# An S4 convolution block and a gated MLP on one core: LayerNorm arithmetic taken off GpSimd, inverse transforms in other PSUM banks, a new schedule

## The chip, the cores and the metric

One core of a Trainium2 chip runs the whole program as one launch. The metric is device time in microseconds (us). The kernel before takes 370.67 us (median of 3 runs, 370.54 to 370.81). Engines in the profile: PE is TensorE (PEld its weight loads), DVE is VectorE, ACT is ScalarE, POOL is GpSimd, SP the queue that issues DMAs. In these traces an engine takes its instructions in the order of its queue: in the kernel before, ACT stood still for 6.19 us behind one result from GpSimd. The order is fixed when the kernel is built: a list scheduler places instructions by priorities that the kernel gives it.

All runs quoted are of the undisturbed state.

## The reference, cut to what matters

```python
def reference(A_u, A_A_re, ..., B_w_gate, B_w_up, B_w_down):
    x = A_u                                      # 1 x 2048 x 640, bf16
    h  = x + _A_ref(_layernorm(x), ...)          # per-channel convolution with a kernel of 2048 taps
    h2 = h + _B_ref(_layernorm(h), ...)          # (sigmoid(ln @ w_gate) * (ln @ w_up)) @ w_down, F = 1728
    return h2
# _A_ref: K = Re(sum_n C exp(dt A l) dt B); y = irfft(rfft(u) * rfft(K)); y + u * Dskip
```

## The kernel before

The sequence is cut into four blocks of 512. In a **setup** of some 157 us the kernel builds tables (sines and exponentials on ACT, products on DVE), normalises the four input blocks (LayerNorm 1), transforms them (`ps_z`), builds the spectra of the convolution kernel (`pk`, `ps_kv`, `ps_xk`) and finishes block 0. Then comes an **MLP stage** of some 212 us, block by block: gate and up projections, down projection; beside them DVE multiplies spectra for the next block (`products`) and PE transforms them back (`inverse`).

LayerNorm 1 before. Block 3's first three rows are summed on ACT (`SA[3]` is 3), and three tiny operations on 3 columns join the sums on GpSimd. Then GpSimd adds eps, takes the power -1/2, and for rows that ACT normalises also forms -mean*rstd:

```python
def ln_stats_act(src, mv, rr, junk, eng=nc.vector, eps=0.0):      # called with nc.gpsimd for LayerNorm 1
    rs = slice(rr[0], rr[-1] + 1)
    for i, r in enumerate(rr):
        nc.scalar.activation(junk(i), src(r), AF.Identity, accum_out=acc[:, 0, r:r + 1])       # L399
    eng.tensor_scalar(acc[:, 0, rs], acc[:, 0, rs], -1.0 / D, None, ALU.mult)                   # L400
    for i, r in enumerate(rr):
        nc.scalar.activation(junk(i), src(r), AF.Square, bias=acc[:, 0, r:r + 1], accum_out=acc[:, 1, r:r + 1])  # L402
    eng.tensor_scalar(mv[:, rs, 0], acc[:, 0, rs], -1.0, None, ALU.mult)                        # L403
    eng.tensor_scalar(mv[:, rs, 1], acc[:, 1, rs], 1.0 / D, eps, ALU.mult, ALU.add)             # L404

def norm(b):
    rs = slice(4 * b, 4 * b + 4); na = AT["NA"][b]
    nc.gpsimd.tensor_scalar(rstd[:, rs], mv[:, rs, 1], 1e-5, None, ALU.add)                     # L416
    nc.gpsimd.tensor_tensor(rstd[:, rs], rstd[:, rs], mhalf[:, rs], ALU.pow)                    # L417
    if na:
        nc.gpsimd.tensor_tensor(nmr[:, rs], mv[:, rs, 0], rstd[:, rs], ALU.mult)                # L419
        nc.gpsimd.tensor_scalar(nmr[:, rs], nmr[:, rs], -1.0, None, ALU.mult)                   # L420
    # ... the last na rows are normalised on ACT, the others on DVE
```

The inverse of a later block goes through the same two PSUM buffers as the up projection, 320 columns at a time, from chunk 9 of 13 on. Blocks in `R4` combine two half spectra on DVE first (radix 4), so that their inverse needs half the matmuls:

```python
def inverse(b, psp):                      # psp = psu_p, two banks of one buffer each
    for half in range(2):
        for s in range(4):
            ps = psp.tile([P, 512], F32, name="ps_y1", tag="ml_pu")
            for ft in range(1 if b in R4 else 2):
                for ri in range(2):
                    MM(ps[:, 0:UH], lhsT=iv(s, ft, ri), rhs=VR[b][...], ...)
            nc.scalar.copy(tb, ps[:, 0:UH]); V(hv, tb, hv, ALU.add)
            yield
# in the MLP loop:
for ft in range(FT):
    up(pg, Wg, 128 * ft); up(pu, Wu, 128 * ft)       # sigmoid, copy, product follow
    if ft > 8: drain(inv, 2)
```

The numbers in `AT` say when each unit of the setup is offered to the scheduler.

## Time and profile before

| | PE | DVE | ACT | POOL |
|---|---|---|---|---|
| busy us of 371.0 | 330.1 | 289.0 | 246.4 | 25.3 |

The table of busy time by stage and the stall at 42 us are shown in the prediction. Two more rows of the page, each a row of 40 slices of 9.3 us, with the busy share (or the granted clock) in tenths:

```profile
PE   1488649896999989989999999998999999999995
...
POOL 1240453100000000010000100000100001000000
PEclk9999969998999999999999999999999999999999
```

Read them above each other: PE's deepest dip after the first 20 us is in the fifth and sixth slice (6 and 4), where POOL is busiest (4 and 5), and the clock has its lowest digit, 6, in the sixth.

One caution for all comparisons of traces: the traced execution of this kernel took 372.78 us, 2.1 more than its median.

### The profile page before, as it was taken

The numbers are of one execution on the slowest core, as the hardware profiler recorded it, in microseconds if no ns is written. First come the engines' busy times: TensorE is split into PE (matmuls) and PEld (weight loads), VectorE is DVE, ScalarE is ACT, GpSimd is POOL, SyncE is SP. The second block draws the span as 40 slices with busy tenths as digits, with TensorE's granted clock in tenths as the row PEclk, the third lists the DMA queues.
The fourth block names the chain that finished last, engine by engine and source line by source line (L and its number), as shares of the span: only waits on it lengthen the run. The fifth ranks groups of instructions, "written<-read, shape, count | busy, mean of one in ns | idle before, by whom it ended". The sixth has DMA issues, their size and how long they took to land.

```text
span 371.0 us, 6647 instructions
## 1 busy us (share of the span) xinstructions
PE 330.1 (89%) x2587; PEld 206.1 (56%) x2602; DVE 289.0 (78%) x594; ACT 246.4 (66%) x450; POOL 25.3 (7%) x32
## 2 busy tenths in 40 slices
PE   1488649896999989989999999998999999999995
PEld 1375436566867677964445654445654436644463
DVE  2979975897899997989999999999999962111221
ACT  6879659897898974476568855558845468755500
POOL 1240453100000000010000100000100001000000
PEclk9999969998999999999999999999999999999999
DMA  7980000146305216979910044000012000010001
GB/s 189 350 331 18 0 2 0 46 144 238 73 2 133 84 72 202 345 203 329 294 65 3 0 144 141 2 0 0 3 71 73 0 0 2 0 72 1 0 30 43
DMA packets 29217, 34.35 MB, mean 93 GB/s; under 512 B 16385, under 2 KB 24578, under 8 KB 28930
## 3 DMA queue, kind: packets, MB, share of 16 engines
q1 hardware_dynamic: 29186, 33.94, 28.2%
q8 instruction: 20, 0.33, 0.4%
q14 instruction: 11, 0.09, 0.1%
HBM read 24.74 MB, written 9.18 MB: 91 GB/s over the span
## 4 chain that ended last, share of the span: by engine, by line
DVE 31%; PE 28%; issue 17%; ACT 16%; POOL 4%; DMA 3%; SPq 1%; POOLq 0%; DVEq 0%; ACTq 0%
PE ml_po L891 5%; DVE u L675 5%; DVE u L674 5%; PE ps_xk L501 4%; PE ml_pu L861 4%; PE ml_pg L861 4%; DVE u L677 3%; DVE u L678 3%; DVE ml_hm L872 2%; PE ps_z L440 2%; PE ps_kv L470 2%; ACT zs L441 2%; ACT a_cs L267 2%; POOL ln_acc L400 2%; PE pk L459 2%
## 5 line engine op out<-in xcount | busy, mean ns | idle before, releaser
L861 PE MATMUL ml_pg<-lnT,Wg 128*128 128x512 bf16 x250 | 65.2, 379 | 0.5
L861 PE MATMUL ml_pu<-lnT,Wu 128*128 128x512 bf16 x256 | 63.7, 379 | 0.2
L891 PE MATMUL ml_po<-Wd,ml_hm 128*128 128x320 bf16 x416 | 59.5, 299 | 0.0
L891 PEld LDWEIGHTS <-ml_hm 128*128 128x128 bf16 x416 | 40.2, 98 | 17.1 <-issue 1.3
L869 ACT ACTIVATE ml_sg<-ml_pg 128x512 bf16<-128x512 f32 x52 | 31.1, 597 | 27.3 <-PE ml_pg L861 15.2
L871 ACT CAST ml_ub<-ml_pu 128x512 bf16<-128x512 f32 x52 | 30.4, 584 | 20.8 <-PE ml_pu L861 19.8
L861 PEld LDWEIGHTS <-Wu 128*128 128x128 bf16 x260 | 25.4, 98 | 30.9 <-issue 0.3
L872 DVE TENSOR_TENSOR ml_hm<-ml_ub,ml_sg 128x512 bf16<-128x512 bf16 x52 | 21.7, 418 | 24.5 <-ACT ml_ub L871 24.5
L440 PE MATMUL ps_z<-u,c_G 128*128 128x320 bf16 x192 | 31.1, 306 | 10.8 <-ACT tabMB L267 6.6
L861 PEld LDWEIGHTS <-Wg 128*128 128x128 bf16 x260 | 25.4, 98 | 26.7
L501 PE MATMUL ps_xk<-kv,c_KM 128*128 128x160 bf16 x320 | 28.6, 241 | 2.6 <-ACT zs L441 1.9
L440 PEld LDWEIGHTS <-c_G 128*128 128x128 bf16 x192 | 18.6, 99 | 20.7 <-issue 11.2
L675 DVE TENSOR_TENSOR u<-Z,S 128x1280 bf16<-128x1280 bf16 x34 | 27.7, 815 | 0.0
L674 DVE TENSOR_TENSOR u<-Z,S 128x1280 bf16<-128x1280 bf16 x34 | 27.5, 814 | 0.0
L240 PE MATMUL ps_t<-fr,c_dg 128*128 128x160 f16 (+1 forms) x180 | 21.0, 247 | 6.7 <-ACT fr L223 4.9
L501 PEld LDWEIGHTS <-c_KM 128*128 128x128 bf16 x320 | 24.2, 102 | 4.4 <-issue 3.6
L240 PEld LDWEIGHTS <-c_dg 128*128 128x128 f16 x180 | 15.7, 103 | 14.5 <-issue 8.6
L410 POOL TENSOR_TENSOR rstd<-mv,mhalf 128x4 f32<-128x4 f32 x4 | 5.1, 1267 | 235.6 <-DVE mv L404 149.7
L677 DVE TENSOR_TENSOR u<-u,u 128x1280 bf16<-128x1280 bf16 x23 | 18.8, 816 | 0.0
L678 DVE TENSOR_TENSOR u<-u,u 128x1280 bf16<-128x1280 bf16 x23 | 18.8, 816 | 0.0
L441 ACT CAST zs<-ps_z 128x640 bf16<-128x640 f32 x24 | 16.4, 721 | 2.0 <-DMA dz<-zs 1.8
L760 PE MATMUL ps_y<-VR,c_IV 128*128 128x320 bf16 x64 | 15.4, 301 | 2.5 <-ACT ml_ub L871 2.3
(156 smaller groups left out, 582.5 us busy)
## 6 DMA issues: line engine op xcount, KB each, us to landing
dz<-zs SPq DMA_DIRECT2D x12, 320.0 KB, 2.2
c_KM<-s4c_KM SPq DMA_DIRECT2D x1, 2560.0 KB, 12.7
h<-in_A_u_dram SPq DMA_DIRECT2D x4, 640.0 KB, 4.4
dxk<-xk SPq DMA_DIRECT2D x16, 160.0 KB, 2.9
eo<-dz SPq DMA_DIRECT2D x4, 640.0 KB, 4.4
S<-dxk SPq DMA_DIRECT2D x4, 640.0 KB, 5.3
Wg<-in_B_w_gate_dram SPq DMA_DIRECT2D x4, 520.0 KB, 8.2
Wu<-in_B_w_up_dram SPq DMA_DIRECT2D x4, 520.0 KB, 8.1
```

The lines of the kernel that those rows point to most:

```text
L240: MM(ps[:, a, q * w:q * w + w], lhsT=dg[:, dk, :], rhs=fr[:, src, i, o + oo:o + oo + w], start=False, stop=(q == m - 1 and i == 1))
L440: MM(ps[:, ri, 0:UH], lhsT=G[:, ft, 0 if b in EO else hf, ri, r, :], rhs=us[b][:, r, o:o + UH], start=(r == rr[0]), stop=(r == rr[-1]))
L501: mm = MM(ps[:, hf, ri * W:ri * W + W], lhsT=KM[:, ft, hf, ri, KI[d] + q, :], rhs=kv[:, j, :], start=(q == 0), stop=(q == len(KD[d]) - 1)).ins
L674: V(t1, z, k[:, :, :, hs_], ALU.mult)
L675: V(t2, z, k[:, :, ::-1, hs_], ALU.mult)
L677: V(s1, s1, t1, ALU.add)
L678: V(s2, s2, t2, ALU.add)
L861: nc.tensor.matmul(ps[:], lhsT=W[:, dc, f0:f0 + 128], rhs=lnT[:, dc].rearrange("p a b -> p (a b)"), start=(dc == 0), stop=(dc == 4))
L869: nc.scalar.activation(sg[:], pg[:], AF.Sigmoid)
L871: nc.scalar.copy(ub[:], pu[:])
L872: nc.vector.tensor_tensor(hm[:, ft, :], ub[:], sg[:], ALU.mult)
L891: nc.tensor.matmul(po[k][:, c, 0:320], lhsT=hm[:, ft, 128 * lr:128 * lr + 128], rhs=Wd[:, ft, 320 * c:320 * c + 320], start=(start and ft ...
```

## The change

The intent, as the diff lets one read it: because of the port that GpSimd shares with VectorE (the page of the Trainium skill is in the prediction), GpSimd keeps only the operation that VectorE is not used for (the power), and the statistics and coefficients go to VectorE. The inverses leave the up projection's banks for those of the down projection, which are idle until it starts. Block 3 loses radix 4. The down eviction is split in two. Most schedule numbers are new.

```diff
-R4 = (1, 3)
+R4 = (1,)
-AT = {"eb": -20.4, ... "NG": (1, 0, 0, 0), "NA": (0, 3, 3, 1), "SA": (0, 0, 0, 3), ...}
+AT = {"eb": -21.2, ... "NG": (1, 0, 0, 1), "NA": (1, 1, 0, 2), "SA": (2, 0, 0, 3), ...}   # most numbers differ
+    def coef(b):
+        rs = slice(4 * b, 4 * b + 4)
+        nc.vector.tensor_scalar(mv[:, rs, 1], mv[:, rs, 1], 1e-5, None, ALU.add)
+        nc.gpsimd.tensor_tensor(rstd[:, rs], mv[:, rs, 1], mhalf[:, rs], ALU.pow)
     def norm(b):
-        nc.gpsimd.tensor_scalar(rstd[:, rs], mv[:, rs, 1], 1e-5, None, ALU.add)
-        nc.gpsimd.tensor_tensor(rstd[:, rs], rstd[:, rs], mhalf[:, rs], ALU.pow)
         if na:
-            nc.gpsimd.tensor_tensor(nmr[:, rs], mv[:, rs, 0], rstd[:, rs], ALU.mult)
-            nc.gpsimd.tensor_scalar(nmr[:, rs], nmr[:, rs], -1.0, None, ALU.mult)
+            nc.vector.scalar_tensor_tensor(nmr[:, qs], mv[:, qs, 0], -1.0, rstd[:, qs], ALU.mult, ALU.mult)
-            ln_stats_act(..., lambda i: junk[:], nc.gpsimd)
+            ln_stats_act(..., lambda i: junk[:])
-        unit(f"n{b}", f"st{b}", L(norm, b))
+        unit(f"w{b}", f"st{b}", L(coef, b))
+        unit(f"n{b}", f"w{b}", L(norm, b))
     def inverse(b, psp):
-            for s in range(4):
-                ps = psp.tile([P, 512], F32, name="ps_y1", tag="ml_pu")
+            for a in range(2):
+                ps = psp.tile([P, 2, 512], F32, name="ps_y1", tag="ml_po")       # two outputs per tile and eviction
-        inv = inverse(b + 1, psu_p)
+        inv = inverse(b + 1, pso_p)
-            if ft > 8: drain(inv, 2)
+            if ft in (7, 8, 10, 12): drain(inv, 1)
-    # down eviction: one ACT copy and one DVE add of 640 columns
+    # down eviction: for c in range(2): one copy and one add of 320 columns
```

## The prediction

> **What bounds the kernel now.** I read the page first (busy shares and the row of 40 slices), then the table of busy time by stage, then the waits of each engine by stage, and last the timeline of the places that stood out. The page gives TensorE (PE) 330.1 us busy of 371, VectorE (DVE) 289.0, ScalarE (ACT) 246.4, GpSimd (POOL) 25.3. In the table of stages (start:end, length, then busy us of PE, PEld, DVE, ACT, POOL, the PE clock, DMA share, GB/s):
>
> ```profile
> 20.00:40.00 20.00, 16.12 (x121) 12.06 (x121) 17.88 (x40) 17.50 (x24) 3.84 (x4) 1.00 0.33 131
> 40.00:60.00 20.00, 12.47 (x88) 8.50 (x88) 16.82 (x41) 12.42 (x22) 11.88 (x11) 0.83 0.01 1
> 60.00:80.00 20.00, 18.53 (x208) 12.29 (x206) 15.36 (x24) 18.83 (x35) 1.15 (x2) 1.00 0.17 64
> 80.00:100.00 20.00, 17.04 (x219) 14.21 (x217) 16.27 (x39) 16.80 (x35) 0.00 (x0) 0.91 0.50 158
> 100.00:120.00 20.00, 19.13 (x216) 14.82 (x216) 19.87 (x37) 17.42 (x26) 0.00 (x0) 1.00 0.27 68
> ...
> 280.00:300.00 20.00, 19.66 (x91) 8.54 (x91) 19.86 (x39) 10.63 (x20) 0.00 (x0) 1.00 0.04 16
> 300.00:320.00 20.00, 19.54 (x138) 11.90 (x138) 5.67 (x20) 16.82 (x35) 1.01 (x1) 1.00 0.00 1
> ```
>
> From 100 us on PE runs at 18 to 20 of every 20 us at full clock: the gate/up/down matmuls, with the far spectra and the inverses as filling. Time there is PE work, with DVE nearly as full up to 300 us. Before 100 us PE is idle 28.2 us (100 less 7.60, 16.12, 12.47, 18.53, 17.04) and DVE 20.7 us. So a gain has to come mainly from the first 100 us. The worst stage is 40 to 60, the only one where GpSimd is busy for long and the only one before 80 us with the PE clock below 1. The timeline shows why:
>
> ```profile
> 42.37 6.93 POOL L400 TENSOR_SCALAR ln_acc<-ln_acc 128x3 f32<-128x3 f32 x1 [17.29 <-ACT junk L399]
> 49.34 0.83 ACT L402 ACTIVATE junk<-u,ln_acc 128x640 bf16<-128x640 bf16 x1 [6.19 <-POOL ln_acc L400]
> 51.16 2.29 PE L440 MATMUL ps_z<-u,c_G 128*128 128x320 bf16 x8 [6.58 <-ACT tabMB L267]
> 51.14 0.66 DVE L298 TENSOR_TENSOR tabMB<-tabEB,tabMB 128x960 bf16<-128x960 bf16 x1 [1.94 <-ACT tabMB L267]
> ```
>
> One GpSimd multiply of 3 columns takes 6.93 us. ACT, in order, waits 6.19 us for it before the squares of block 3's statistics; a cosine table behind them comes late; PE, needing its PSUM tile, waits 6.58 us. DVE had other work and loses only 1.94 us at once. The debt comes later: before 59.61 us DVE waits 1.2 us for a GpSimd pow of the late block 3 or its neighbour, and in 60 to 80 us 4.6 us in one piece for table A's buffer, held by late PE products.
>
> **What the skill says.** "SBUF — State Buffer", section "Who interferes with whom": GpSimd's SBUF port is DVE's second pair, an exclusive lock; a DVE instruction with two SBUF inputs blocks a GpSimd instruction that reads SBUF. The trace agrees: from 42.97 to 49.2 us DVE ran two-input TENSOR_TENSORs without a gap, and the GpSimd multiply ended at 49.30, when DVE ran dry. The same kind of operation took 0.24 us at 49.38, and the multiply of 1.70 us at 23.37 ended just after a 1.48 us DVE product from 23.51. "TensorE: Matmul & The Clock Gate", section "HAM oscillation — how this bites in real kernels": an idle gap over about 3.4 us drops the clock. Here, after 6.58 idle us, eight 320-column matmuls took 2.29 us against 1.25 us for the eight at 26.94, and two groups of six 160-column matmuls 1.00 us each against 0.58. Same page, "Back-to-back issue gap": N/2.4 + 2.5 ns, so 136 ns at N = 320; the trace has 26 down matmuls in 3.69 us, 142 ns each.
>
> **The change, part by part.**
>
> (1) *GpSimd keeps only pow.* The three operations of L400, L403, L404, four +eps (L416) and three multiply pairs (L419, L420) leave GpSimd; DVE gets some 13 tiny operations, mostly in place of longer GpSimd ones, 0.1 to 0.2 us each (the tiny aggregates of L394 are 0.196), so about +2 us of DVE. The pows stay (L417, 1.05 us each). They can still be blocked, but nearly all that follows a pow is now DVE's own: when DVE reaches the normalisation it stops, the port comes free, and the pow ends in about 1 us. Starvation limits itself. On the path: 6.58 us of PE wait go, and some 1.9 us of slow clock (1.04 for the eight plus 0.42 twice). Together 8.5 us at most. Not all comes back, because DVE must keep up: of its own idle time from 40 to 100 us, waits of 1.94, 1.2, 4.6, 2.1 and 1.4 us, 11.2 us in all, I let the 7.7 us that follow from the stall (1.94 + 1.2 + 4.6) be recoverable, less the 2 us added. I take **5.5 us**.
>
> (2) *New schedule numbers and shares.* Block 0 gets two rows of statistics on ACT, ACT normalises 4 rows instead of 7, and the negation of the last table goes to ACT. DVE: two fewer rows of statistics at 2x0.464 + 0.196 = 1.12 each, -2.2; three more normalised rows at 0.43, +1.3; negation of two half tables, about -1: **-2 us of DVE**, cancelling the addition of (1). ACT: two rows at (0.73 + 0.82 + 2x0.19), +3.9; three rows at 0.926, -2.8; negation at half the 2.39 us of the whole table, twice, +2.4: +3.5 us, on an engine with 36% idle. The order of the whole setup is redone; block 1's normalisation and block 3's forward transform move forward, the last chunk's kernel products back. No row tells what an order is worth. As it was surely searched with (1) in place, and PE still has 15 idle us in 0 to 40, I choose **+1.5 us of gain**.
>
> (3) *Inverses to the down projection's banks.* Eight 320-wide tiles per block in the two-buffer up-projection banks become four 2x320 tiles in banks idle until the down projection, issued after chunks 7, 8, 10 and 12 instead of 9 to 12. PE's waits of L760 on ACT's up evictions, 2.3 us in four, should go. ACT: 24 copies at 0.429 become 12 at 0.682 (the down eviction of the same shape), 10.3 to 8.2; DVE: 24 adds at 0.317 become 12 at 0.486, 7.6 to 5.8. I take **2 us**.
>
> (4) *Block 3 without radix 4.* PE: 4 outputs, 2 halves and 2 products more: 16 more 320-column matmuls at 0.14 = **2.2 us lost** on the bound engine. DVE: 4 x (0.482 + 0.482 + 0.317) = 5.1 us less in products(3), which end near 301 us. That helps only if inverse(3) must not be waited for earlier; PE waits just 0.2 us for VR there now, so I count 0.
>
> (5) *Down evictions in halves.* 12 ACT copies at 0.682 become 24 at 0.429, +2.1 us; 12 DVE adds at 0.486 become 24 at 0.317, +1.8. Both cancel (3)'s savings and lie beside PE's work. At the end, the last 0.82 us add from PSUM becomes two of about 0.45, the first starting one matmul (0.14) earlier: 0 ± 0.1.
>
> Sum: 5.5 + 1.5 + 2 - 2.2 = 6.8 us, less a little for worse fits: 370.7 to about **363.6 us**, -1.9%.
>
> **Rivals.**
> A. *The stall moves.* Pow at block 3 or the new ACT statistics of block 0 wait in turn: ACT now needs DVE to reach a tiny multiply in its own queue, and pow can be starved. For it: pow reads two SBUF inputs; four pows in the second half take 1.0 to 1.5 us and DVE waits about 1 us for each. Against: none of eight pows exceeded 1.51 us. If several waits of 1 to 2 us appear the gain shrinks to some 3 us: 367 to 368.
> B. *DVE becomes the bound.* It is 99% busy from 100 to 120 us and 95 to 100% in every stage from 160 to 300 us, so an earlier PE might just wait for it at the inverses, which now come two chunks earlier. For it: the chain of waits runs almost wholly over DVE from 145 to 260 us. Against: DVE loses 5.1 us of radix 4, and its 20.7 idle us before 100 are of the same order as PE's. If it holds, the stall's gain is halved: 365 to 366.
> C. *The reordering is worth more.* PE has 28 idle us before 100; if the new order uses 5 us more of them, with the stall gone, 358 to 360. Nothing in the profile speaks against it but that the first 27 us wait for loads and the phase computation.
> D. *The extra matmuls bite doubly*, with weight loads exposed where inverses are interleaved (pairs at 0.23 us apart now, around the narrow edge matmuls): 16 x 0.23 = 3.7 us instead of 2.2. It adds 1.5 us.
>
> **Range and chances.** The central sum is 363.6. The terms I chose rather than read, (1)'s share and (2), carry ±3 us each, so about ±5: 358 to 368.5. The line of 2% is 363.3, next to the estimate. Slower by 2% would need a new stall of 14 us, which nothing suggests. Faster 0.48, same 0.50, slower 0.02.
>
> **What would show it.** (1) is right if no GpSimd operation lasts over 2 us, PE's wait on the cosine table is gone, the clock stays 1.00 in 40 to 60 us and PE is busy there for 16 us or more. (2): PE's idle time before 100 us falls from 28 to about 20 us. (3): the inverse matmuls wait under 0.5 us in all. (4): 80 instead of 64 inverse matmuls, 2 us more PE work, DVE through products(3) earlier relative to the end of PE's work. (5): the tail after the last matmul stays near 0.8 us plus the store. It is wrong if PE's idle time before 100 us hardly changes (A), if inverses wait for VR (B), or if far more than 8 us of it goes (C).

## The result

After: 366.11 us median of 4 runs (365.43 to 367.81), beside 370.74 us (370.54 to 370.85, 4 runs) of the kernel before. The ratio is 0.9883 with a 95% interval of 0.9849 to 0.9916: about 1.2% faster, inside 2%. Ratios here are the mean time of one kernel's runs over that of the other's of the same rounds, so not quite the ratio of the medians. The prediction's range, 358.0 to 368.5, holds the result; its central value, 363.6, was 2.5 us too low.

The stage table of the kernel after (columns as in the prediction: start:end, length, busy us of PE, PEld, DVE, ACT, POOL, PE clock, DMA share, GB/s):

```profile
20.00:40.00 20.00, 15.97 (x108) 10.76 (x108) 18.54 (x49) 18.68 (x28) 2.02 (x2) 0.91 0.29 117
40.00:60.00 20.00, 17.64 (x213) 12.43 (x215) 20.00 (x48) 17.73 (x35) 2.75 (x2) 1.00 0.01 2
60.00:80.00 20.00, 16.85 (x160) 11.40 (x149) 19.80 (x42) 18.39 (x36) 0.92 (x1) 1.00 0.43 148
80.00:100.00 20.00, 18.20 (x235) 13.87 (x234) 16.27 (x31) 19.15 (x31) 0.00 (x0) 1.00 0.28 85
...
280.00:300.00 20.00, 20.00 (x103) 9.20 (x102) 10.80 (x22) 11.46 (x21) 0.00 (x0) 1.00 0.00 0
```

From 40 to 60 us PE does 17.64 us of work instead of 12.47, at full clock, and DVE never stops. From 280 to 300 us DVE is done with its products half way through, where it was full before (part of this is only that the whole MLP stage begins 7.3 us earlier, see below). GpSimd's timeline (start us, duration us, engine, line, operation) now holds four powers of LayerNorm 1 and nothing long:

```profile
21.29 1.01 POOL L416 TENSOR_TENSOR rstd<-mv,mhalf 128x4 f32<-128x4 f32 x1 [19.79 <-DVE mv L415]
27.17 1.01 POOL L416 TENSOR_TENSOR rstd<-mv,mhalf 128x4 f32<-128x4 f32 x1 [4.87 <-DVE mv L415]
44.66 1.18 POOL L416 TENSOR_TENSOR rstd<-mv,mhalf 128x4 f32<-128x4 f32 x1 [16.47 <-DVE mv L415]
55.67 1.57 POOL L416 TENSOR_TENSOR rstd<-mv,mhalf 128x4 f32<-128x4 f32 x1 [9.84 <-DVE mv L415]
```

A good marker splits every trace in two: the start of the first power of LayerNorm 2 (L410), after which the MLP stage runs. It stands at 158.83 us before (about 156.7 in a run of median length, if its 2.1 us surplus is taken off) and at 151.51 us after. From there to the end it is 212.17 us before and 212.69 us after. So the whole gain, about 5 us, was made in the setup, and the MLP stage gave half a microsecond back.

### The profile page after: what moved, and what is told of

It is laid out like the page before. It is cut to its first block, busy times and chain, and to the rows that moved or that the text cites. A ratio compares the mean times of both kernels' runs of the same rounds, so it can differ in the third digit from the quotient of the medians.

```text
span 364.2 us, 6687 instructions
## 1 busy us (share of the span) xinstructions
PE 330.4 (91%) x2618; PEld 205.6 (56%) x2618; DVE 284.4 (78%) x594; ACT 249.4 (68%) x457; POOL 11.1 (3%) x19
## 4 chain that ended last, share of the span: by engine, by line
PE 39%; DVE 32%; ACT 20%; issue 3%; DMA 3%; POOL 1%; SPq 1%; POOLq 0%; DVEq 0%; ACTq 0%
PE ml_pg L867 8%; PE ml_pu L867 8%; PE ml_po L900 6%; DVE u L679 5%; DVE u L678 5%; DVE u L682 3%; DVE u L681 3%; ACT zs L444 3%; PE ps_xk L504 2%; DVE ml_hm L878 2%; PE ps_kv L473 2%; PE pk L462 2%; ACT a_sn L267 2%; DVE VR L689 2%; PE ps_z L443 2%
## 5 line engine op out<-in xcount | busy, mean ns | idle before, releaser
L875 ACT ACTIVATE ml_sg<-ml_pg 128x512 bf16<-128x512 f32 x52 | 31.0, 597 | 24.2 <-PE ml_pg L867 16.3
L443 PE MATMUL ps_z<-u,c_G 128*128 128x320 bf16 x192 | 29.1, 298 | 4.7 <-ACT zs L444 2.8
L504 PE MATMUL ps_xk<-kv,c_KM 128*128 128x160 bf16 x320 | 27.1, 232 | 1.9 <-ACT xk L508 0.8
L504 PEld LDWEIGHTS <-c_KM 128*128 128x128 bf16 x320 | 22.8, 98 | 4.3 <-issue 3.0
L462 PE MATMUL pk<-tabB,tabA 128*128 128x84 bf16 x320 | 15.5, 200 | 2.7 <-ACT kts L463 2.6
L462 PEld LDWEIGHTS <-tabA 128*128 128x128 bf16 x320 | 14.0, 97 | 6.0 <-issue 3.6
L463 ACT CAST kts<-pk 128x420 bf16<-128x420 f32 x32 | 15.0, 533 | 2.9 <-PE pk L462 2.9
```

Of the source, the lines that this page charges most:

```text
L443: MM(ps[:, ri, 0:UH], lhsT=G[:, ft, 0 if b in EO else hf, ri, r, :], rhs=us[b][:, r, o:o + UH], start=(r == rr[0]), stop=(r == rr[-1]))
L462: MM(pk[:, i, :], lhsT=A[:, ri, g].rearrange("p e c -> p (e c)"), rhs=B[:, ri, :, 4 * g:4 * g + 4], start=(ri == 0), stop=(ri == 1))
L504: mm = MM(ps[:, hf, ri * W:ri * W + W], lhsT=KM[:, ft, hf, ri, KI[d] + q, :], rhs=kv[:, j, :], start=(q == 0), stop=(q == len(KD[d]) - 1)).ins
L875: nc.scalar.activation(sg[:], pg[:], AF.Sigmoid)
```

## The experiments

Twelve runs were made beside the before and the after, all correct. "Setup" is the time to that marker in the traced run, "rest" from there to the end of the span; each is one execution, not a median.

| run | what it is | median us (range) | ratio to before (95%) | setup | rest |
|---|---|---|---|---|---|
| before | | 370.67 (370.54 to 370.81) | | 158.83 | 212.17 |
| after | | 366.11 (365.43 to 367.81) | 0.9883 (0.9849 to 0.9916) | 151.51 | 212.69 |
| b_stats | before, statistics of block 3 on DVE | 365.48 (365.27 to 367.57) | 0.9869 (0.9828 to 0.991) | 153.41 | 212.39 |
| b_part1 | before, whole GpSimd part | 372.11 (371.95 to 372.21) | 1.0036 (0.9998 to 1.0074) | 158.09 | 212.11 |
| b_order | before, new schedule alone | 371.72 (370.19 to 372.19) | 1.0017 (0.9979 to 1.0056) | 156.03 | 212.37 |
| b_part3 | before, inverses in down banks | 371.36 (370.76 to 371.80) | 1.0014 (0.998 to 1.0047) | 156.74 | 212.96 |
| b_hole | before, one superfluous DVE instruction | 370.00 (369.18 to 371.38) | 0.9977 (0.994 to 1.0013) | 157.38 | 212.22 |
| b_act | before, the stalled multiply on ACT | 365.29 (364.00 to 365.92) | 0.9841 (0.9806 to 0.9877) | 150.89 | 212.11 |
| a_r4 | after, radix 4 back for block 3 | 367.07 (365.85 to 367.43) | 0.9888 (0.9855 to 0.9921) | 153.32 | 212.28 |
| a_no3 | after, inverses back in up banks | 366.59 (365.95 to 367.44) | 0.9875 (0.984 to 0.9911) | 151.85 | 213.75 |
| b_p1order | before, GpSimd part and new schedule | 365.04 (364.12 to 365.38) | 0.9851 (0.9825 to 0.9878) | 150.46 | 211.84 |
| b_p1e | before, GpSimd part, three old numbers changed | 363.30 (362.71 to 363.65) | 0.9804 (0.9778 to 0.983) | 149.48 | 212.12 |
| b_act2 | as b_act, other two operations on DVE | 366.86 (365.33 to 367.73) | 0.9899 (0.9866 to 0.9932) | 152.99 | 212.11 |
| after_again | after, unchanged | 365.44 (364.79 to 366.44) | 0.9867 (0.9839 to 0.9894) | 150.34 | 212.66 |

The rows from b_stats to b_part3 shared their rounds, as did b_hole to a_no3, and the last four; the medians of before were 370.43, 371.10 and 370.41 us there.

**b_stats: is it the stall?** Only the word that put block 3's three statistics operations on GpSimd goes; some of the setup's order shifts with it.

```diff
-            ln_stats_act(ur, mv, range(4 * b + n, 4 * b + 4), lambda i: junk[:], nc.gpsimd)
+            ln_stats_act(ur, mv, range(4 * b + n, 4 * b + 4), lambda i: junk[:])
```

> Kernel before, with only the three tiny operations of block 3's ScalarE statistics moved from GpSimd to VectorE; old schedule numbers. Theory 'stall' (the 6.93 us GpSimd multiply is the loss): PE's wait of 6.58 us on the cosine table disappears, no GpSimd operation over 2 us remains, and the time falls by 4 to 6 us, to 365 to 367 us. Rival 'order' (the gain of the change came from the re-searched schedule, and the stall was hidden by other work): the wait disappears but the time falls by less than 1.5 us, or other waits of the same sum appear before 100 us.

Measured: 365.48 us, ratio 0.9869. One word gives as much as the whole change. How it does so is worth a look, in ACT's and DVE's timelines of this run:

```profile
51.09 0.16 DVE L400 TENSOR_SCALAR ln_acc<-ln_acc 128x3 f32<-128x3 f32 x1
...
51.35 0.83 ACT L402 ACTIVATE junk<-u,ln_acc 128x640 bf16<-128x640 bf16 x1
```

PE's longest wait from 40 to 60 us on ACT's cosine table is now 0.3 us. The multiply itself is *later* than before (51.09, against an end at 49.30 on GpSimd). But the squares now stand behind other work in ACT's queue, so ACT does not wait for them, and neither does PE. What was removed is not latency but a wait in an in-order queue.

**b_part1: the whole GpSimd part under the old order.** The diff is the part of `coef`, `norm`, the statistics and the `w` units shown above; each new number `w` equals the old `n` of its block (2.5, 22.2, 62.0, 81.6).

> Kernel before with the whole GpSimd part of the change (only pow left there; coefficients and normalisation as two scheduled units), old shares and schedule numbers. 'Stall': about as the statistics alone or a little better, 364.5 to 366.5 us. 'Order': 369 us or more, because the old order does not fit the new units.

Measured: 372.11 us, no gain at all, if anything 0.4% slower. The stall at 42 us is gone and another has come. From its timelines of DVE and PE:

```profile
53.71 0.48 DVE L393 BATCH_NORM_STATS2 ln_st<-u 128x6 f32<-128x320 bf16 x1
...
65.82 0.19 DVE L394 BATCH_NORM_AGGREGATE mv<-ln_st 128x2 f32<-128x12 f32 x1
...
70.33 0.16 DVE L415 TENSOR_SCALAR mv<-mv 128x4 f32<-128x4 f32 x1
...
72.42 0.16 DVE L423 SCALAR_TENSOR_TENSOR nmr<-mv,rstd 128x3 f32<-128x3 f32 x1 [0.90 <-POOL rstd L416]
...
73.00 3.44 PE L443 MATMUL ps_z<-u,c_G 128*128 128x320 bf16 x12 [10.93 <-DVE u L428]
```

The last statistics of block 2 are taken at 53.71, but aggregated only at 65.82, behind a row of table products. Then the +eps, which now belongs to DVE, waits until 70.33 behind further products; the rows are ready at about 73, and PE has waited 10.93 us. In the kernel before the same aggregate ran at 57.38 on DVE and the +eps at 57.66 on GpSimd. So of the 12.7 us by which the +eps is later, 4.5 us are its own wait in DVE's queue; 8.4 us come from the aggregate, which was DVE's before too and which the scheduler has now placed later. A moved operation waits in the queue of its new engine, and the move also reorders operations that did not move.

**b_order: the new schedule numbers alone.**

```diff
-AT = {"eb": -20.4, "ea0": -15.3, ...}
+AT = {"eb": -21.2, "ea0": -13.4, ...}      # the whole table of the kernel after; code and R4 as before
```

> Kernel before with the new schedule numbers and shares alone; norm and statistics still on GpSimd, inverses in the up banks, radix 4 for block 3. 'Order': 365 to 367 us. 'Stall': GpSimd operations of several us are still there, now with block 0's statistics too, and the time is 370 us or more.

Measured: 371.72 us, nothing gained. The lock strikes elsewhere, in GpSimd's timeline:

```profile
46.52 7.90 POOL L403 TENSOR_SCALAR mv<-ln_acc 128x3 f32<-128x3 f32 x1
```

Here it has waiters: the coefficients that follow it on GpSimd are done at 57.14, ACT waits 2.09 us for them and PE 3.13 us for the copies that stand behind them on ACT. The new order is worth nothing while the coefficients stay on GpSimd.

**b_part3: the inverses in the down banks alone.** The diff is that of `inverse`, `inv` and `drain` above.

> Kernel before with only the inverses of blocks 1 to 3 in the down projection's PSUM banks, two column halves of an output pair per tile. Prediction: PE's waits at the inverses on the up evictions (2.3 us) go, 368.5 to 369 us. Rival: PE has other work that fills these waits or DVE sets the pace there, so under 0.5 us, 370.3 us or more.

Measured: 371.36 us, ratio 1.0014: nothing. PE's waits in the MLP stage, kernel before, then this one (who waited for whom: us in total, times, longest; `ml_ub` is the copy of an up result, `ln` a normalised row):

```profile
PE ps_y L760 <- ACT ml_ub L871: 2.3, 4, 1.5
PE ml_pt L834 <- ACT ln L820: 0.9, 2, 0.6
```

```profile
PE ml_pt L836 <- ACT ln L822: 1.8, 4, 0.6
PE ml_po L893 <- ACT Wd L913: 0.8, 1, 0.8
```

The waits of the inverses on the up evictions, 2.3 us, are gone as predicted. But PE then waits 0.9 us more for the normalised rows of the next block, which come at the end of DVE's and ACT's chain, and 0.8 us for a down bank still being evicted. The new waits are smaller than the 2.3 us, and yet the rest became 0.8 us longer. The trace shows one reason: 24 down matmuls at 266.17 took 4.70 us, against 3.42 us for 24 in the kernel after, in the only part of this rest where the granted clock was clearly below 1 (0.93 from 261 to 266 us, 0.72 from 266 to 271). Whether the change caused that stretch is not shown. That the time does not fall by 2 us is shown by the runs.

**b_hole: is it really the port?** A superfluous DVE instruction with one SBUF input is put into the row of two-input products during which the multiply had waited. Up to there DVE's order is that of the kernel before; GpSimd keeps everything.

```diff
-            V(dst[:, 1], dst[:, 1], t[:, 0], ALU.add)
+            V(dst[:, 1], dst[:, 1], t[:, 0], ALU.add); (c or d0 != 8) or nc.vector.bn_stats(hole[:], dst[:, 1, 0:2].rearrange("p n w -> p (n w)"))
```

> Kernel before plus one superfluous VectorE statistics instruction (one SBUF input, 320 columns, 0.44 us, result unused) in the first B chain, in the middle of the row of two-input VectorE products during which the 6.93 us GpSimd multiply waited, at about 46.4 us; GpSimd keeps all its work. Lock theory: the GpSimd multiply ends when that instruction runs, after about 4 us instead of 6.93, and PE's wait on the cosine table falls from 6.58 to about 3.7 us, although VectorE has more to do; time 368 to 369.5 us. Rival (the multiply is slow for GpSimd's own reasons, a cold start for instance): it stays at 6 to 7 us and the time stays at 370.5 us or more.

Measured: 370.00 us, ratio 0.9977, not clear of no change; the mechanism shows in the timelines of GpSimd, DVE and PE all the same:

```profile
41.81 4.12 POOL L400 TENSOR_SCALAR ln_acc<-ln_acc 128x3 f32<-128x3 f32 x1 [17.30 <-ACT junk L399]
...
50.03 2.69 POOL L404 TENSOR_SCALAR mv<-ln_acc 128x3 f32<-128x3 f32 x1 [3.78 <-ACT junk L402]
```

```profile
45.34 0.49 DVE L380 TENSOR_TENSOR tabB<-tabB,tabMB 128x640 bf16<-128x640 bf16 x1
45.74 0.49 DVE L386 BATCH_NORM_STATS2 hole<-tabB 128x6 f32<-128x320 bf16 x1
46.15 0.88 DVE L380 TENSOR_TENSOR tS<-tabB,tabMB 128x640 bf16<-128x640 bf16 x2
```

```profile
47.79 2.29 PE L440 MATMUL ps_z<-u,c_G 128*128 128x320 bf16 x8 [3.77 <-ACT tabMB L267]
...
57.21 0.57 PE L245 MATMUL ps_t<-ones,mg 128*128 128x480 f16 x2 [2.96 <-ACT a_sn L267]
```

The multiply ends at 45.93 (41.81 + 4.12), 0.19 us after the one-input instruction begins, while in the kernel before it ran on to 49.30. PE's wait on the cosine table is 3.8 us instead of 6.6. Adding work to DVE made GpSimd faster. The rival, a slow GpSimd of its own, has fallen. But the time hardly moved, because the next GpSimd operation, L404, was then caught for 2.69 us by the following row of products, until the next one-input instruction (52.57); ACT waited 2.59 us for block 3's coefficients and PE 2.96 us for ACT. The two PE waits, 3.8 and 3.0 us, make up the old 6.6.

**b_act: the one multiply on ACT.** ACT makes the sums, so the multiply follows in its own queue and waits for nobody.

```diff
-        eng.tensor_scalar(acc[:, 0, rs], acc[:, 0, rs], -1.0 / D, None, ALU.mult)
+        (nc.scalar.mul(acc[:, 0, rs], acc[:, 0, rs], -1.0 / D) if eng is nc.gpsimd else eng.tensor_scalar(...))
```

> Kernel before with only the stalled multiply (negated mean, 3 columns) on ScalarE, in order behind its own sums; the other two statistics operations stay on GpSimd. Stall theory: like the move to VectorE, 365 to 367 us, unless the next two GpSimd operations are starved in turn. Rival (the gain of that move lay in moving all three, or in the accompanying reordering): 369 us or more.

Measured: 365.29 us, ratio 0.9841. GpSimd's next operation now took longer than any other, in its timeline beside DVE's:

```profile
42.57 9.60 POOL L403 TENSOR_SCALAR mv<-ln_acc 128x3 f32<-128x3 f32 x1 [18.25 <-ACT ln_acc L400]
```

```profile
51.67 0.40 DVE L386 TENSOR_TENSOR tabB<-tabB,tS 128x480 bf16<-128x480 bf16 x1
51.99 0.49 DVE L393 BATCH_NORM_STATS2 ln_st<-u 128x6 f32<-128x320 bf16 x1
```

It ends at 52.17, again just after a one-input instruction begins (51.99). One wait in this trace looks like its work and is not: ACT stands 2.48 us (until 58.02) for block 2's coefficients from GpSimd, and PE 2.02 us behind it. But GpSimd had finished the coefficients behind the blocked operation (block 3's) by 54.76, and block 2's last aggregate was ready only at 54.79, so the chain that ACT waited for began no later for it. So 9.60 us blocked cost nothing that the trace or the time shows, while 6.93 us with ACT behind it had cost 5 to 6.

**a_r4: what block 3's radix 4 is worth in the kernel after.**

```diff
-R4 = (1,)
+R4 = (1, 3)
```

> Kernel after with radix 4 for block 3 again. Prediction's step (4): 16 matmuls of 0.14 us less on the bound engine, so 2.2 us faster than after, 363.5 to 364.5 us. Rival (VectorE's 5.1 us more of products(3) make the inverse wait): the same as after or slower, and PE waits for VR.

Measured: 367.07 us, ratio 0.9888, against 0.9883 of the kernel after in other rounds: no difference. The rest is 212.28 against 212.69 us, so 0.4 us of the expected 2.2. PE's work is indeed less (its 64 inverse matmuls take 13.6 us, the 80 of the kernel after 15.6). What is missing stands for the most part in PE's waits between 260 and 320 us (`VR` is DVE's product of the spectra):

```profile
PE ps_y L766 <- DVE VR L751: 1.6, 1, 1.6
```

With the inverses two chunks earlier, DVE's radix-4 combination comes too late by 1.6 us. The kernel after has no such wait.

**a_no3: the inverses back in the up banks, rest as after.** The diff is the inverse of that of b_part3.

> Kernel after with the inverses back in the up projection's banks, chunks 9 to 12. Prediction's step (3): PE waits 2 us more at the inverses, 368 us. Rival (what the banks save is lost again to waits for LayerNorm or for a down bank, as the one-part kernel showed): within 0.7 us of after, 365.5 to 366.8 us.

Measured: 366.59 us, ratio 0.9875, as good as after by time. In the trace the rest grew by 1.1 us (213.75 against 212.69): PE waits 2.1 us on up evictions again, and less for LayerNorm rows (0.6 instead of 1.9 us). But the same 26 down matmuls, first here and then in the kernel after, show another difference:

```profile
246.15 5.37 PE L898 MATMUL ml_po<-Wd,ml_hm 128*128 128x320 bf16 x26
```

```profile
243.29 3.69 PE L900 MATMUL ml_po<-Wd,ml_hm 128*128 128x320 bf16 x26
```

The granted clock was 0.83 from 242 to 252 us here and 1.00 in the kernel after. That stretch alone took 1.7 us more. It follows a wait of 1.8 us on an up eviction, but waits of 1.5 us (before) and 2.0 us (b_p1order) at the same place were not followed by one, and in b_stats a like stretch goes with a rest of 212.39 us. So neither the times nor this trace show that the banks are worth anything.

**b_p1order: GpSimd part and new schedule together.** Diff: b_part1's code with b_order's table.

> Kernel before with the GpSimd part and the new schedule numbers together; inverses in the up banks, whole down evictions, radix 4 for block 3. Each of the two alone gained nothing. Theory 'they only work together': 365.5 to 367 us, all of the change's gain. Rival (the inverses' banks and block 3's radix supply it): 369 us or more.

Measured: 365.04 us, ratio 0.9851, beside 0.9867 of the kernel after in the same rounds. Two parts that gain nothing alone give everything together. What this kernel lacks (down banks, no radix 4 in block 3, split evictions) brings nothing on top by these runs; its rest is 211.84 against 212.66 us of `after_again`.

**b_p1e: the moved operations earlier in the queue.** As b_part1, with three numbers changed, so that DVE reaches block 2's +eps some 30 instructions earlier:

```diff
-"st2": 63.5, ... "w2": 62.0, "w3": 81.6
+"st2": 40.0, ... "w2": 41.0, "w3": 45.0
```

> The GpSimd part with old schedule numbers again, but statistics and coefficients of blocks 2 and 3 at 40, 41 and 45 instead of 63.5, 62 and 81.6, so that VectorE reaches block 2's +eps some 30 instructions earlier. In the first try the +eps stood in VectorE's own queue behind a chain of products and PE waited 10.9 us for the normalised rows. Theory 'a moved operation takes its place in the new engine's queue': that wait falls below 3 us and the time is 364.5 to 367 us. Rival (the GpSimd part is a loss under the old order for another reason): 370 us or more.

Measured: 363.30 us, ratio 0.9804 (0.9778 to 0.983), the fastest kernel: faster than before by 2.0% (the interval includes 2%, so whether it passes that line is unclear) and than the kernel after of the same rounds by 2.1 us in the medians, the ranges apart (362.71 to 363.65 against 364.79 to 366.44). DVE's timeline has the aggregate of block 2 at 52.25 instead of 65.82 and its +eps at 52.56 instead of 70.33, and GpSimd's power follows at once:

```profile
52.56 0.16 DVE L415 TENSOR_SCALAR mv<-mv 128x4 f32<-128x4 f32 x1
...
53.83 0.16 DVE L423 SCALAR_TENSOR_TENSOR nmr<-mv,rstd 128x3 f32<-128x3 f32 x1 [0.75 <-POOL rstd L416]
```

PE's wait of 10.93 us is gone; the longest single one from 40 to 80 us is 1.5 us. The rival has fallen. Since the statistics, which had not moved, were brought forward together with the +eps, the run shows that the order was at fault, not which of the two mattered more.

**b_act2: the other two operations on DVE as well.**

```diff
+        eng = nc.vector      # behind the multiply of b_act
```

> Kernel before with the stalled multiply on ScalarE and the other two statistics operations of block 3 on VectorE. When these two stayed on GpSimd one of them took 9.60 us, yet the time fell as far. Theory 'a blocked operation costs only what waits for it': within 1 us of that kernel, 364.3 to 366.3 us. Rival: the 9.6 us did cost, and this kernel is 2 us or more faster, below 363.5 us.

Measured: 366.86 us, ratio 0.9899, slower than b_act was in its rounds and on neither expectation. The two operations brought another order with them, and PE waits for block 2's rows:

```profile
67.72 12.25 PE L440 MATMUL ps_z<-u,c_G 128*128 128x320 bf16 x72 [4.03 <-DVE u L425]
```

In b_act PE had no such wait; its normalised row was ready at about 57 us, here at 67.65. So this run settles nothing about the 9.60 us; what speaks there is b_act itself, which gained all that had been lost with the 9.60 us in it.

**after_again.**

> Kernel after, unchanged, so that it stands in the same rounds as the three above: 365.5 to 367 us; if the one-operation move is as good as the whole change, within 1 us of the kernel beside it.

Measured: 365.44 us (364.79 to 366.44). b_p1order lies 0.4 us below it, not clear of it.

## Why the prediction came out as it did

The bound was read rightly: all gain lay before the MLP stage, and the MLP stage stayed at 212 to 213 us in nearly every kernel, whatever was done to it. PE's idle time before 100 us went from 28.2 to 22.3 us; "about 20" had been forecast. The signs named for (1), (3) and (4) came: no GpSimd operation above 1.57 us in LayerNorm 1, the wait on the cosine table gone, 17.64 us of PE work at full clock from 40 to 60 us, no wait at the inverses, 80 inverse matmuls with 2.0 us more work than 64. The sum of the prediction holds small slips: 370.7 less 6.8 is 363.9, not 363.6; ACT is idle for 34% of the span by the page (and 19% before 100 us), not 36%; and PE's idle time from 0 to 40 us is 16.3 us, not 15. Step by step:

- **Step (1), the stall.** Right in mechanism, shown by b_hole (the multiply ends when DVE runs a one-input instruction) and by b_stats and b_act (the time falls by 1.3 and 1.6% when the multiply leaves GpSimd). Its 5.5 us was about right for the multiply alone (371.10 to 365.29 in b_act) and for the three statistics together (370.43 to 365.48 in b_stats). The slow clock went from 40 to 60 us but came back from 20 to 40 us (0.91 in the kernel after). What was not seen is that the rest of step (1), the coefficients on DVE, could cost as much again: b_part1 lost it all to a wait of 10.93 us. The sentence that DVE reaches the normalisation and stops looked at the lock and not at how long DVE takes to get there. This is rival A, "the stall moves", in a form that was not named: into DVE's own queue, and to operations that the scheduler places anew.
- **Step (2), the schedule.** Its 1.5 us was added to (1) as if the two were independent. They are not: b_order gives nothing, b_part1 gives nothing, both give 5.4 us by the medians of the same rounds (370.41 to 365.04). Forecast for both: 7.0 us. This difference of 1.6 us is one of the three terms that were mis-sized; the others, in (3) and (4), nearly cancel. b_p1e, with 7.1 us, shows that such an order existed. The number was saved by the remark that the order "was surely searched with (1) in place": under the old order (1) gains nothing, so the total stood on an order of which no row of the profile told.
- **Step (3), the banks.** The waits of 2.3 us went, as said: no inverse matmul in the kernel after waits for an eviction. The gain of 2 us did not follow: 0 in b_part3 and 0 by time in a_no3 (the 1.1 us of its trace go with a stretch of slow clock). In the kernel after PE met DVE's and ACT's chain at the next LayerNorm (1.9 us) and at the narrow last chunk (0.9 us). That is rival B in its mild form.
- **Step (4), radix 4.** The loss of 2.2 us was too large. Matmul time did grow by 2.0 us (15.6 for 80 inverse matmuls, 13.6 for 64 in a_r4), but keeping radix 4 costs a wait of 1.6 us for VR in the new order (a_r4), so its loss is 0.4 us by trace. The step's "I count 0" for DVE's 5.1 us looked at the wait in the old order, 0.2 us, while step (3) of the same change brought the inverses forward.
- **Step (5), the evictions.** Not tested alone. At the end of the program the last add takes 0.89 us in two halves against 0.82 before, as forecast; the first half did not start a matmul earlier.
- **Rivals.** C and D did not occur: PE's idle time fell less than forecast, and no run gave a sign of the extra matmuls costing more than was put down. (3), (4) and (5) together were put at 0.2 us lost and came out, by b_p1order against after_again, at 0.4 us lost by the medians and 0.8 by the traces.

What stays open: whether the kernel after is slower than b_p1order at all (the intervals overlap), why identical kernels differ by up to 2.4 us between executions (365.43 to 367.81 for after), what the stretches of slow clock in single traces come from, and what the down banks are worth, also under b_p1e's order.

## What to carry to other kernels

A blocked operation costs what waits for it and no more: first ask who stands behind it in whose queue, then move the one operation that has a waiter, to the engine that makes its input if possible. When work moves to a busy in-order engine, look at where it lands in that engine's order and what else the move has reordered; a part that loses alone may need three numbers changed, not dropping. And do not book the removal of a wait as a gain: in b_part3 2.3 us of waits went and the time did not fall.

## What the Trainium skill lacked or had wrong

- "SBUF — State Buffer", section "Who interferes with whom", describes the lock for one instruction against one. It doesn't say that a GpSimd operation stays out through a whole row of DVE instructions back to back: 6.93 us before, 7.90 in b_order, 9.60 in b_act for 3 columns, work that takes 0.24 us when free. It ended 0.17 to 0.19 us after a one-input DVE instruction began (b_hole, b_act, b_order), or when DVE ran dry (before), each time 0.09 to 0.10 us after the end of the last product in the row. It is not always so: in the kernel before, two GpSimd operations at 53.41 and 54.12 ended after 0.63 and 0.50 us in the middle of an unbroken row of two-input products (51.14 to 54.77). What decides between the two is not shown.
- The same section's statement that a DVE instruction with one SBUF input outside the 2-port modes doesn't contend agrees with b_hole; the use of such an instruction as a way in for GpSimd is on no page.
- "TensorE: Matmul & The Clock Gate", section "HAM oscillation — how this bites in real kernels", gives idle gaps over about 3.4 us as what slows the clock. Read alone, it would not have foretold the following. In the kernel before, twelve 160-column matmuls after a gap of 1.94 us at 90.04 us took 1.76 us against 0.99 at 150.19; in the kernel after, six took 1.01 us at 26.55 us against 0.58 at 29.42, after gaps of no more than 1.06 us in a half-idle stretch. Gaps of like length differ: in b_p1order the 26 down matmuls that followed one of 2.02 us (ended 243.68) took 3.69 us, in a_no3 behind one of 1.81 us at the same place 5.37 us.
